# Polysketch attention into a squared-ReLU FFN: the first batch's later denominators from extra sketch columns, and its first q sketch ahead of the first FFN matmul

## The chip, the core and the metric

The kernel runs on one core of a Trainium2 chip. The metric is the device time of one execution in microseconds (us). The engines are TensorE (PE; PEld is its weight load), VectorE (DVE), ScalarE (ACT), GpSimd (POOL) and SyncE (SP, which here only issues DMAs).

## What is computed

The attention has a product feature map. Each vector x of 32 numbers is sketched by S1 and S2 into a and b of 8 numbers each, and the feature vector holds all 64 products of an entry of a with an entry of b. Its output, with the four heads side by side, is the input of a two-layer FFN with a squared ReLU.

```python
def phi(x):                                   # S1, S2: 8 x 32
    a = np.einsum('rd,bhsd->bhsr', S1, x)
    b = np.einsum('rd,bhsd->bhsr', S2, x)
    return np.einsum('bhsi,bhsj->bhsij', a, b).reshape(*x.shape[:-1], 64)
q_p, k_p = (phi(q), phi(k))                   # q, k, v: 4 batches, 4 heads, 1088 rows, 32
kv = np.einsum('bhsf,bhsd->bhfd', k_p, v)
z = np.sum(k_p, axis=2)
num = np.einsum('bhsf,bhfd->bhsd', q_p, kv)
den = np.einsum('bhsf,bhf->bhs', q_p, z)[..., None] + 1e-06
attn = num / den
x = attn.transpose(0, 2, 1, 3).reshape(4352, 128)
h = np.maximum(x @ w_in, 0.0)                 # w_in: 128 x 2048
out = h * h @ w_out                           # w_out: 2048 x 128
```

The denominator can be written in a second way: den is the sum over i of a_i(q) times (the sum over j of z_ij S2_j) applied to q. So a sketch of q with eight more columns, one for each i, gives the second factor directly.

## The kernel before

The four batches (b = 0 to 3) are pipelined: while the FFN of one batch runs, the attention of the next is made. The FFN works on chunks of columns of xT (the attention's output, 128 features by tokens). For b = 0 the chunks (list `FC`) are 256, 384 and 448 columns. Each chunk goes through 16 slices d of the hidden width: a first matmul `pg` (L615, weights `w_in`), a ReLU on ACT (L624), a square on ACT (L632) or DVE (L634), and a second matmul `po` (L653, weights `w_o`, two records each). One to four slices that fit into 512 columns are a unit. `pg` has two buffers, so the first matmuls of a unit wait for the ReLU of the unit two before.

`w_in` comes by DMA in four pieces of 512 columns, and POOL casts each piece (L689, `cast_wi`) to the type that the first matmul reads. Piece c serves the slices 4c to 4c+3: d = 0 to 3 need piece 0, d = 8 to 11 need piece 2, d = 12 to 15 need piece 3.

The attention of b = 0 has its own start, written out by hand. Its first chunk (256 tokens) is made by a short path: `kf` and `kp` (k features), `kvp` (the sums kv and z, 36 matmuls, L376), `x` (q features, L749), `bd` (kv and z as block-diagonal weights, L780), `den` and `num` (L795), then on DVE `dT` (L804), `rd`, `bc` and `xT` (L810). `a_rep` (L419) copies kv to all partitions through PE into the tile `x0`, and ACT takes it to SBUF as `kv` (L425). `keep_warm` (L696) issues matmuls whose result isn't used. The tile `x0` and the later `qc`, `kc`, `nd` and `kvp` tiles share one PSUM buffer of four banks (tag `att`, one buffer).

The rest of b = 0 is two chunks (list `AC`: (8, 12) and (20, 16), in blocks of 32 tokens; 384 and 576 tokens with padding), and b = 1 to 3 are one chunk each. For a chunk: `qT` (L289) transposes q on DVE, `qc` (L296) is the sketch on PE, six shuffles `qb` and `qa` (L506) and four products `qp` (L521) on DVE make the features, and `nd` (L538) is num on PE. The denominator is made in two ways:

- For b = 0, eight more matmuls against `z0` (L547) follow in the same PSUM tile; DVE transposes the result (`dT`, L561), adds eps (L563) and inverts it (L569). `z0` is made once by DVE (`a_rep_z`, L431) with the mask `own_c`.
- For b = 1 to 3, the sketch has eight more columns (`sw`, columns 16 to 23, made by `a_w`, L455 and L461). DVE transposes the sketch (`qt`, L469), multiplies (`pd`, L476), sums with eps (L486) and inverts (`rc`, L490). POOL then lays the result out with 16 small copies (`rd`, L497, `a_rl`).

In both cases `bc` (L575) spreads the inverse and `xT` (L584) is num times it.

Everything after the start goes through a planner (`_Order`). Each operation has an engine, a price, a key, needs, buffers and sometimes a time before which it must not start (`at`). The planner simulates the engines, takes on each free engine the ready operation with the lowest key, and emits all of it in that order. Each engine then executes its own instructions strictly in the emitted order. The operation `wi` of pieces 2 and 3 of `w_in` is one of them:

```python
for c in (2, 3):
    O.add(("wi", c), {"POOL": 0.7}, 0.5 * c, [], on(cast_wi, c), at=WI[c - 2])   # WI = (1.5, 3.0)
```

DMAs are issued by SP in program order[...].

Of the kernel before, what the change touches and what calls it, by code (L numbers as in the profile page):

```python
# [104 lines left out]
def kernel(  # L105
# [21 lines left out]
    W0, W3 = 10, 3  # L127
# [37 lines left out]
    z0 = sb("z0", 64 * H)  # L165

# [59 lines left out]
    for p in range(4):  # L226
        load_v(nc.sync, 0, p, 4, NT)
    load_wi(nc.sync, 0)
    load_wi(nc.sync, 1)
    load_q(nc.sync, 0, 256, S)  # L230
# [22 lines left out]
    own_c, own_p = sb("own_c", 32), sb("own_p", 2)  # L253
    nc.vector.memset(own_c[:], 0.0)
# [3 lines left out]
    for h in range(H):  # L258
        nc.vector.memset(own_c[32 * h : 32 * h + 32, 8 * h : 8 * h + 8], 1.0)
# [170 lines left out]
    def a_rep_z(t_, col):  # L430
        nc.vector.tensor_tensor(  # L431
            out=_ap(z0, 0, 128, 0, [[32, 4], [128, 2], [1, 32]]),
            in0=_ap(t_, 0, 128, col + 32, [[512, 4], [64, 2], [1, 32]]),
            in1=_ap(own_c, 0, 128, 0, [[0, 4], [0, 2], [1, 32]]),
            op=mult,
        )

# [10 lines left out]
    def a_qc(b, i0, nb):  # L448
        st[b, "qc", i0] = att("qc")
        sketch(st[b, "qc", i0], qT, 32 * i0, 8 * nb, sw[b % 2] if b else sf[:, 64:96])  # L450
# [14 lines left out]
    def a_qt(b, x):  # L465
        if x == 0:
            st[b, "qt"] = wpool.tile([128, 32 * NT * H], F32, tag="qt", bufs=1, name="qt")
        m = 32 * NT
        nc.vector.transpose(  # L469
            _ap(st[b, "qt"], 0, 128, 2 * m * x, [[m, 2], [1, m]]),  # L470
            banks(st[b, "qc", 0], 2 * x, 0, m),
        )

    def a_pd(b):
        qt = st[b, "qt"]
        nc.vector.tensor_tensor(  # L476
            out=_ap(pd, 0, 128, 0, [[9, 4 * NT], [1, 8]]),
            in0=_ap(qt, 0, 128, 0, [[32, 4 * NT], [1, 8]]),
            in1=_ap(qt, 0, 128, 16, [[32, 4 * NT], [1, 8]]),
            op=mult,  # L480
        )


    def a_rc(b):
        dn = wpool.tile([128, 4 * NT], F32, tag="dn", name="dn")
        nc.vector.tensor_reduce(  # L486
            out=dn[:, :], in_=_ap(pd, 0, 128, 0, [[9, 4 * NT], [1, 9]]), op=add, axis=AX
        )
        st[b, "rc"] = wpool.tile([128, 4 * NT], F32, tag="rc", bufs=1, name="rc")
        nc.vector.reciprocal(st[b, "rc"][:, :], dn[:, :])  # L490


    def a_rl(b, c):
        if c == 0:
            st[b, "rd", 0] = wpool.tile([128, 4 * NT], F32, tag="rd", name="rd")
        for h in range(H):
            nc.gpsimd.tensor_copy(  # L497
                st[b, "rd", 0][32 * h : 32 * h + 32, NT * c : NT * c + NT],
                st[b, "rc"][32 * c : 32 * c + 32, NT * h : NT * h + NT],
            )  # L500
# [26 lines left out]

    def a_nd(b, i0, nb, nd=None, col=0):
        m = 8 * nb
        nd = att("nd") if nd is None else nd  # L530
        st[b, "nd", i0] = nd, col
        kv, z = st[b, "kv"], z0
        for e in range(E):
            qp = st[b, "qp", i0, e]
            ch = [(c, h) for c in range(4) for h in range(H)]
            for c, h in ch:
                r, o = slice(32 * c, 32 * c + 32), 64 * h + 32 * e
                nc.tensor.matmul(  # L538
                    nd[32 * h : 32 * h + 32, 512 * c + col : 512 * c + col + m],
                    kv[r, o : o + 32], qp[r, m * h : m * h + m],  # L540
                    start=(e == 0), stop=(e == 1),
                )
        for o_, m0, w in dens(m) if b == 0 else ():
            for e in range(E):
                for h in range(H):
                    o = 64 * h + 32 * e
                    nc.tensor.matmul(  # L547
                        nd[32 * h : 32 * h + 32, col + o_ : col + o_ + w],
                        z[:, o : o + 32], st[b, "qp", i0, e][:, m * h + m0 : m * h + m0 + w],
                        start=(e == 0), stop=(e == 1),  # L550
                    )

    def dens(m):
        return [(m, 0, m)]

    def a_dn(b, i0, nb):
        m = 8 * nb
        (nd, col), q4 = st[b, "nd", i0], nb // 4
        dT = wpool.tile([128, 32 * NT], F32, tag="dT", bufs=1, name="dT")
        for o_, m0, w in dens(m):  # L560
            nc.vector.transpose(dT[:, m0 : m0 + w], nd[:, col + o_ : col + o_ + w])  # L561
        dn = wpool.tile([128, 4 * NT], F32, tag="dn", name="dn")
        nc.vector.tensor_scalar(  # L563
            out=_ap(dn, 0, 128, 0, [[q4, 4], [1, q4]]),
            in0=_ap(dT, 0, 128, 0, [[8, 4], [32, q4]]),
            scalar1=1e-6, scalar2=None, op0=add,
        )
        rd = st[b, "rd", i0] = wpool.tile([128, 4 * NT], F32, tag="rd", name="rd")
        nc.vector.reciprocal(rd[:, 0:nb], dn[:, 0:nb])  # L569
# [10 lines left out]
    def a_x(b, i0, nb, x, k=2):  # L580
        m = 8 * nb
        if (b, "xT") not in st:
            st[b, "xT"] = bpool.tile([128, SP], F32R, tag="xT", name="xT")
        nc.vector.tensor_tensor(  # L584
            out=_ap(st[b, "xT"], 0, 128, 32 * i0 + 2 * m * x, [[m, k], [1, m]]),
            in0=banks(st[b, "nd", i0][0], 2 * x, st[b, "nd", i0][1], m, k),
            in1=_ap(st[b, "bc", i0], 0, 128, 2 * m * x, [[m, k], [1, m]]),
            op=mult,
        )
# [137 lines left out]
    iden, irep = sb("iden", 128), sb("irep", 128)  # L727
    make_identity(nc, iden[:])
# [27 lines left out]
    a_kf(4, 3, psf, "po")  # L756
    q0(0)
# [3 lines left out]
    for t0, n in ((0, 2), (2, 2), (4, 3), (7, 2)):  # L761
        a_kp0(t0, n)
        for t in range(t0, t0 + n):
            a_kv0(t)
        if t0 == 0:
            a_kf(7, 2, psf, "po")
# [5 lines left out]
    for y in range(2):  # L772
        nc.tensor.matmul(  # L773
            den0[64 * y : 64 * y + 64, 0:256], eps[0:1, 0:64], eps[0:1, 64:320],
            start=True, stop=False,
        )

    bd = sb("bd", 256)
    for x in (1, 0):
        nc.vector.tensor_tensor(  # L780
            out=_ap(bd, 0, 128, 128 * x, [[64, 2], [32, 2], [1, 32]]),
            in0=_ap(st[0, "kvp"], 0, 128, 32 * x, [[64, 2], [0, 2], [1, 32]]),
            in1=_ap(own_p, 0, 128, 0, [[0, 2], [1, 2], [0, 32]]),
            op=mult,
        )
    st["kvt"] = wpool.tile([128, 128], F32, tag="kvt", name="kvt")
    nc.scalar.copy(st["kvt"][:, :], st[0, "kvp"][:, 0:128])
# [5 lines left out]
    for t_, x in ((den0, 1), (num0, 0)):  # L793
        for y in range(2):
# [3 lines left out]
            )  # L798
    a_rep(x0, 256)
    st["warm"] = psf.tile([128, 512], F32, tag="po", name="warm")  # L800
    keep_warm(W3)
    a_rep_kv(x0, 256)
# [10 lines left out]
    a_rep_z(x0, 256)  # L813
# [26 lines left out]
    def q_tasks(b, i0, nb, key):  # L840
# [4 lines left out]
        if True:  # L845
            for x in range(2):
# [7 lines left out]
                )  # L854
        O.add(
            ("qc", b, i0), {"PE": 0.75}, k0 - 1.0, names + [("w", b)], on(a_qc, b, i0, nb),
            rings=[("att", 1)], lag=PEL,
        )
        prev["qTuse"] = [("qc", b, i0)] if i0 + nb == 4 * NT else []
        if b:  # L860
            for x in range(2):
                O.add(
                    ("qt", b, x), {"DVE": dve(m)}, k0 - 0.3 + 0.1 * x, [], on(a_qt, b, x),
                    uses=[("qc", b, i0)], rings=[("qt", 1)] if x == 0 else [],
                )
            O.add(
                ("pd", b), {"DVE": dve(m // 2)}, k0 - 0.1, [("rc", b - 1)], on(a_pd, b),
                uses=[("qt", b, 0), ("qt", b, 1)],
            )
            O.add(  # L870
                ("rc", b), {"DVE": 0.8}, k0 - 0.1, [], on(a_rc, b), uses=[("pd", b)],
                rings=[("rc", 1)],
            )
            for c in range(4):
                O.add(
                    ("rl", b, c), {"POOL": 0.8}, k0 + 0.1 * c, [], on(a_rl, b, c),
                    uses=[("rc", b)], rings=[("rd", 2)] if c == 0 else [],
                )
# [16 lines left out]
    def nd_tasks(b, i0, nb, key):  # L895
# [3 lines left out]
            ("nd", b, i0), {"PE": 1.65 if b else 0.7 + 2.5 * max(nb, 14) / 36}, key - 3.5 - 4 * dve(m), [("kvr", b, h) for h in range(H)], on(a_nd, b, i0, nb),  # L899
            uses=qps + [("qp", b, i0, 0, 0)], rings=[("att", 1)], lag=PEL,  # L900
        )
        if b == 0:
            O.add(
                ("dn", b, i0), {"DVE": 0.72 + m / 960 / 2}, key - 3.0 - 4 * dve(m), [],
                on(a_dn, b, i0, nb), uses=[("nd", b, i0)],
            )
        for x in range(2):
            O.add(
                ("bc", b, i0, x), {"DVE": dve(m)}, key - 2.5 - 4 * dve(m) + 0.1 * x, [], on(a_bc, b, i0, nb, x),
                uses=[("dn", b, i0)] if b == 0 else [("rl", b, 2 * x), ("rl", b, 2 * x + 1)],  # L910
# [88 lines left out]
    for u in range(NU):  # L999
# [8 lines left out]
        for i in range(m):  # L1008
# [13 lines left out]
            tu[u] - 0.6, [],  # L1022
# [65 lines left out]
```

## Time and profile before

| | us |
|---|---|
| runs before: median of 4 | 189.2 (189.17 to 189.69) |
| the profiled execution | 189.12 |
| its span, first to last instruction | 187.3 |
| outside of the span | 1.8 |
| first FFN matmul (`pg`, L615) begins | 14.17 |
| first matmul of slice 12, after the first `nd` | 20.30 |
| last FFN matmuls (`pol`, L648) end in the chain | 183.35 |

The granted TensorE clock was 0.995 of full speed. Times in a timeline are from the start of the span. A line of the timeline has the start, the time, the engine, the line of the kernel, the operation, what it writes and reads, how many are merged, and in brackets the idle time of the engine before it and what ended it. A merged line covers its instructions from the first start to the last end or the sum of their times, so single instructions are shown where a duration matters.

### The profile page before, as it was taken

To read this page: it belongs to the slowest core of one execution; us is meant where nothing else is said; L and a number is where in the kernel's file an instruction comes from. 1 tells how busy PE (TensorE), PEld (TensorE's weight loads), DVE (VectorE), ACT (ScalarE), POOL (GpSimd) and SP (SyncE) were. 2 spreads that over 40 slices of the span, in tenths; PEclk is the share of its full clock that TensorE was granted. 3 is DMA by queue.
4 is the path that set the end of the run, shared out by engine and by line. 5 is a ranking of instruction groups with operands and counts; after the bars stand their busy time and mean duration, and the time that the engine had idled before them with its cause. 6 is when DMAs were issued, how large, how long until landed. Compare 5 with 4: busy or idle time off the path is not lost.

```text
span 187.3 us, 4142 instructions
## 1 busy us (share of the span) xinstructions
PE 181.9 (97%) x1586; PEld 121.9 (65%) x1587; DVE 115.3 (62%) x261; ACT 149.4 (80%) x329; POOL 28.1 (15%) x125
## 2 busy tenths in 40 slices
PE   8999999999999999999999999999999999999991
PEld 2767866666656666656577666656577656666891
DVE  4779879958992589469944589469943412222400
ACT  3418778778978989789698989789699998999960
POOL 2832000028400000085000000085000000000000
PEclk9999999999999999999999999999999999999998
DMA  5799600100039500200069200200020200020100
GB/s 178 167 334 330 161 4 2 28 3 5 0 50 267 127 7 0 44 1 2 6 138 258 37 3 0 42 4 0 5 42 0 35 0 2 8 45 0 31 11 28
DMA packets 24411, 11.27 MB, mean 60 GB/s; under 512 B 17864, under 2 KB 22728, under 8 KB 24392
## 3 DMA queue, kind: packets, MB, share of 16 engines
q1 hardware_dynamic: 23940, 10.82, 23.7%
q8 instruction: 12, 0.20, 0.4%
q10 hardware_dynamic: 452, 0.20, 0.4%
q14 instruction: 7, 0.06, 0.1%
HBM read 8.78 MB, written 2.23 MB: 59 GB/s over the span
## 4 chain that ended last, share of the span: by engine, by line
PE 94%; DMA 2%; DVE 1%; issue 0%; ACT 0%; POOL 0%; ACTq 0%; DVEq 0%
PE po L653 60%; PE pg L615 18%; PE nd L538 3%; PE kvp L394 2%; PE pol L648 2%; PE po L648 2%; PE qc L296 2%; DMA s_nat<-in_S_dram 2%; PE kvp L376 1%; PE kf L306 1%; PE kc L296 1%; PE x L749 1%; PE nd L547 1%; PE den L795 0%; PE den L773 0%
## 5 line engine op out<-in xcount | busy, mean ns | idle before, releaser
L653 PE MATMUL po<-g,w_o 128*128 128x384 f32 (+3 forms) x352 | 138.5, 478 | 0.0
L615 PE MATMUL pg<-xT,w_in 128*128 128x384 f32 (+3 forms) x192 | 110.1, 582 | 0.3 <-DVE xT L810 0.3
L624 ACT ACTIVATE gt<-pg 128x384 f32<-128x384 f32 (+4 forms) x177 | 85.2, 489 | 20.0 <-PE pg L615 16.9
L653 PEld LDWEIGHTS po<-g,w_o 128*128 128x128 f32 x352 | 62.6, 189 | 22.4 <-issue 7.3
L632 ACT ACTIVATE g<-gt 128x384 f32<-128x384 f32 (+3 forms) x138 | 71.0, 532 | 2.9
L615 PEld LDWEIGHTS pg<-xT,w_in 128*128 128x128 f32 x192 | 36.0, 190 | 24.9 <-issue 6.6
L634 DVE TENSOR_TENSOR g<-gt 128x384 f32<-128x384 f32 (+4 forms) x39 | 21.6, 556 | 39.5 <-ACT gt L624 39.4
L443 POOL COPY kv<-kvt 32x64 f32<-32x64 f32 x48 | 11.8, 246 | 90.3 <-PE po L653 63.8
L506 DVE STREAM_SHUFFLE qa<-qc 128x576 f32<-128x576 f32 (+2 forms) x20 | 11.6, 647 | 0.0
L521 DVE TENSOR_TENSOR qp<-qa,qb 128x576 f32<-128x576 f32 (+2 forms) x20 | 10.8, 598 | 0.0
L497 POOL COPY rd<-rc 32x9 f32<-32x9 f32 x48 | 8.9, 185 | 2.1
L347 DVE TENSOR_TENSOR kp<-fs 128x576 f32<-128x576 f32 x12 | 8.2, 742 | 0.0
L469 DVE STREAM_TRANSPOSE qt<-qc 128x576 f32<-128x576 f32 x6 | 4.3, 762 | 5.5 <-PE qc L296 5.5
L657 DVE STREAM_TRANSPOSE oT<-po 128x384 f32<-128x384 f32 (+3 forms) x11 | 6.2, 560 | 1.2 <-PE po L653 1.0
L538 PE MATMUL nd<-qp,kv 32*32 32x288 f32 (+2 forms) x320 | 6.8, 353 | 0.0
L338 DVE STREAM_TRANSPOSE fs<-kc 128x576 f32<-128x576 f32 x6 | 4.3, 762 | 3.9 <-PE kc L296 3.9
L538 PEld LDWEIGHTS nd<-qp,kv 32*32 32x32 f32 x320 | 3.8, 103 | 3.5 <-issue 1.7
L584 DVE TENSOR_TENSOR xT<-nd,bc 128x576 fp32r<-128x576 f32 (+2 forms) x10 | 5.6, 598 | 0.8 <-PE nd L538 0.7
L506 DVE STREAM_SHUFFLE qb<-qc 128x576 f32<-128x576 f32 (+2 forms) x10 | 6.0, 646 | 0.0
L289 DVE STREAM_TRANSPOSE qT<-qn 128x192 f32<-128x192 f32 (+3 forms) x11 | 5.8, 563 | 0.0
L696 PE MATMUL warm<-const-bfloat16-1.0 128*128 128x512 bf16 x12 | 5.0, 571 | 0.8 <-PEq L1072 0.8
L648 PE MATMUL pol<-w_o,g 128*128 128x128 f32 x32 | 5.7, 275 | 0.0
(98 smaller groups left out, 97.5 us busy)
## 6 DMA issues: line engine op xcount, KB each, us to landing
kn<-in_k_dram SPq DMA_DIRECT2D x3, 544.0 KB, 6.2
qn<-in_q_dram SPq DMA_DIRECT2D x3, 544.0 KB, 7.1
vn<-in_v_dram SPq DMA_DIRECT2D x9, 144.0 KB, 5.0
out_dram<-oT SPq DMA_DIRECT2D x24, 48.0 KB, 1.8
w_in<-in_moe_w_in_dram SPq DMA_DIRECT2D x4, 256.0 KB, 5.9
w_o<-in_moe_w_out_dram SPq DMA_DIRECT2D x4, 256.0 KB, 6.6
out_dram<-oT SPq DMA_DIRECT2D x8, 56.0 KB, 1.9
qn<-in_q_dram SPq DMA_DIRECT2D x1, 416.0 KB, 6.2
```

What stands on the lines that cost most here:

```text
L347: nc.vector.tensor_tensor(out=_ap(st[b, "kp"], 0, 128, 2 * o, [[64, NT], [8, 8], [1, 8]]), in0=_ap(fs, 0, 128, o, [[32, NT], [1, 8], [0, 8]]),
L443: nc.gpsimd.tensor_copy(_ap(st[b, "kv"], 32 * c, 32, 64 * h, [[32, E], [1, 32]]), _ap(st["kvt"], 32 * h, 32, 0, [[64, E], [1, 32]]),)
L497: nc.gpsimd.tensor_copy(st[b, "rd", 0][32 * h : 32 * h + 32, NT * c : NT * c + NT], st[b, "rc"][32 * c : 32 * c + 32, NT * h : NT * h + NT],)
L506: nc.vector.stream_shuffle(in_=banks(st[b, "qc", i0], 2 * x, 0, m), out=_ap(st[b, which, i0], 0, 128, 2 * m * x, [[m, 2], [1, m]]), mask=m ...
L521: nc.vector.tensor_tensor(out=st[b, "qp", i0, e][:, r], in0=st[b, f"qa{e}", i0][:, r], in1=st[b, "qb", i0][:, r], op=mult,)
L538: nc.tensor.matmul(nd[32 * h : 32 * h + 32, 512 * c + col : 512 * c + col + m], kv[r, o : o + 32], qp[r, m * h : m * h + m], start=(e == 0 ...
L615: nc.tensor.matmul(st["pg", u][:, n * i : n * i + n], w_in[:, 128 * (d0 + i) : 128 * (d0 + i) + 128], st[b, "xT"][:, c0 : c0 + n],)
L624: nc.scalar.activation(gt[:, 0:w], st["pg", u][:, 0:w], Relu)
L632: nc.scalar.activation(g2[:, 0:w], gt[:, 0:w], Square)
L634: nc.vector.tensor_tensor(out=g2[:, 0:w], in0=gt[:, 0:w], in1=gt[:, 0:w], op=mult)
L648: nc.tensor.matmul(po[x // 128][:, 0:128], g[:, x : x + 128], w, start=(d == 0), stop=(d == NB - 1),)
L653: nc.tensor.matmul(po[0][:, 0:n], w, g, start=(d == 0), stop=(d == NB - 1))
```

## The change

1. **Denominators of the two later chunks of b = 0.** The eight matmuls against `z0`, `z0` itself, the mask `own_c`, and the DVE steps `dT`, add and reciprocal go. Instead the chunks take the way of the other batches: `qc` reads `sw[0]` with eight more columns, then `qt`, `pd`, `rc` on DVE and 16 copies `rl` on POOL for each of the two chunks.
2. **How the extra columns of b = 0 are made.** DVE transposes S2 into `s2f`, `zm` is z with a mask `own_f`, four small matmuls of `s2f` and `zm` go into columns 384 to 391 of `x0`, and ACT copies them to `sw[0]`.
3. **The first q sketch.** `qT` and `qc` of the chunk (8, 12) are issued in the hand-written start: `qT` on DVE before `bd`, `qc` on PE between two `keep_warm` matmuls, ahead of the first `pg`. Three `keep_warm` matmuls become two.
4. **Order of the start.** `kf` of the k tiles 7 and 8 goes ahead of the q features on PE; `kvt` is copied by DVE instead of ACT; `num` goes behind `a_rep`; POOL makes the identity earlier. The second q load is cut in two, and its first part (256 to 640, 192 KB) goes ahead of the first two `w_in` pieces on SP.
5. **Keys.** The squares of the first two units get a much earlier key.

The planner makes a new order from this. On POOL it puts the 16 copies of the chunk (8, 12) ahead of the cast of piece 3 of `w_in`; the cast of piece 2 stays ahead of them:

```
w_in<-w_in 128x512 x3
rd<-rc 32x3 x16
w_in<-w_in 128x512
rd<-rc 32x4 x16
```

On DVE the chunk (8, 12) reads: `xT`, `qt` x2, `pd`, squares 128x256 x2, sum, reciprocal, `qb` x2, `qa` x4, `qp` x4, `bc`, a square 128x512, `bc`, `qT` x2, `xT` x2. On PE, the first `nd` stands behind the same FFN matmuls as before (12 `pg`, 5 `po`), and the second `nd` and what follows it for b = 1 one slice later.

```diff
+    load_q(nc.sync, 0, 256, 640)
     load_wi(nc.sync, 0)
     load_wi(nc.sync, 1)
-    load_q(nc.sync, 0, 256, S)
+    load_q(nc.sync, 0, 640, S)
...
-    own_c, own_p = sb("own_c", 32), sb("own_p", 2)
+    own_p = sb("own_p", 2)
...
+    iden, irep = sb("iden", 128), sb("irep", 128)
+    make_identity(nc, iden[:])
+    own_f, s2f, zm = sb("own_f", 16), sb("s2f", 32), sb("zm", 32)
+    nc.vector.tensor_reduce(
+        out=own_f[:, :], in_=_ap(iden, 0, 128, 0, [[8, 16], [1, 8]]), op=add, axis=AX
+    )
...
-        sketch(st[b, "qc", i0], qT, 32 * i0, 8 * nb, sw[b % 2] if b else sf[:, 64:96])
+        sketch(st[b, "qc", i0], qT, 32 * i0, 8 * nb, sw[b % 2])
...
-    def a_rl(b, c):
+    def a_rl(b, i0, nb, c):
+        n = nb // 4
         if c == 0:
-            st[b, "rd", 0] = wpool.tile([128, 4 * NT], F32, tag="rd", name="rd")
+            st[b, "rd", i0] = wpool.tile([128, 4 * NT], F32, tag="rd", name="rd")
         for h in range(H):
             nc.gpsimd.tensor_copy(
-                st[b, "rd", 0][32 * h : 32 * h + 32, NT * c : NT * c + NT],
-                st[b, "rc"][32 * c : 32 * c + 32, NT * h : NT * h + NT],
+                st[b, "rd", i0][32 * h : 32 * h + 32, n * c : n * c + n],
+                st["rc"][32 * c : 32 * c + 32, n * h : n * h + n],
             )
...
-        for o_, m0, w in dens(m) if b == 0 else ():
-            for e in range(E):
-                for h in range(H):
-                    o = 64 * h + 32 * e
-                    nc.tensor.matmul(
-                        nd[32 * h : 32 * h + 32, col + o_ : col + o_ + w],
-                        z[:, o : o + 32], st[b, "qp", i0, e][:, m * h + m0 : m * h + m0 + w],
-                        start=(e == 0), stop=(e == 1),
-                    )
...
     a_kf(4, 3, psf, "po")
+    a_kf(7, 2, psf, "pg")
     q0(0)
     q0(1)
...
-        if t0 == 0:
-            a_kf(7, 2, psf, "po")
+
+    nc.vector.transpose(s2f[:, :], _ap(sf, 0, 128, 72, [[0, 4], [1, 8]]))
...
+    for i0 in (8, 14):
+        a_qT(0, i0, 6)
...
+    a_bd(1)
     st["kvt"] = wpool.tile([128, 128], F32, tag="kvt", name="kvt")
-    nc.scalar.copy(st["kvt"][:, :], st[0, "kvp"][:, 0:128])
+    nc.vector.tensor_copy(st["kvt"][:, :], st[0, "kvp"][:, 0:128])
+    nc.vector.tensor_tensor(
+        out=_ap(zm, 0, 128, 0, [[16, 2], [8, 2], [1, 8]]),
+        in0=_ap(st[0, "kvp"], 0, 128, 32, [[64, 2], [0, 2], [1, 8]]),
+        in1=_ap(own_f, 0, 128, 0, [[0, 2], [8, 2], [1, 8]]),
+        op=mult,
+    )
+    a_bd(0)
...
+    nd0(den0, 1)
+    for h in range(H):
+        nc.tensor.matmul(
+            x0[32 * h : 32 * h + 32, 384:392], s2f[:, :], zm[:, 8 * h : 8 * h + 8],
+            skip_group_check=True,
+        )
     a_rep(x0, 256)
+    nc.scalar.copy(sw[0][:, 16:24], x0[:, 384:392])
+    a_rep_kv(x0, 256)
+    nd0(num0, 0)
     st["warm"] = psf.tile([128, 512], F32, tag="po", name="warm")
     keep_warm(W3)
-    a_rep_kv(x0, 256)
+    a_qc(0, *AC[0][1])
+    keep_warm(W4)
...
-    a_rep_z(x0, 256)
...
-        if b:
-            for x in range(2):
+        for x in range(2):
...
-                    ("rl", b, c), {"POOL": 0.8}, k0 + 0.1 * c, [], on(a_rl, b, c),
-                    uses=[("rc", b)], rings=[("rd", 2)] if c == 0 else [],
+                ("rl", b, i0, c), {"POOL": 0.8}, k0 + 0.1 * c, [], on(a_rl, b, i0, nb, c),
+                uses=[("rc", b, i0)], rings=[("rd", 2)] if c == 0 else [],
...
-            tu[u] - 0.6, [],
+            tu[u] - (0.6 if u > 1 else 40.0), [],
```

## The prediction

> **What bounds the kernel now.** First the page's busy times and its chain.
>
> ```profile
> PE 181.9 (97%) x1586; PEld 121.9 (65%) x1587; DVE 115.3 (62%) x261; ACT 149.4 (80%) x329; POOL 28.1 (15%) x125
> PE 94%; DMA 2%; DVE 1%; issue 0%; ACT 0%; POOL 0%; ACTq 0%; DVEq 0%
> ```
>
> From the first FFN matmul to the end, PE issues almost without a hole, so the end follows from when PE begins, what it must issue, and where it has to wait. Next, the timeline of the start and of the two `nd` blocks.
>
> ```profile
> 9.27 1.85 PE L376 MATMUL kvp<-vn,kp 128*64 128x64 f32 x56
> 11.17 0.49 DVE L780 TENSOR_TENSOR bd<-kvp,own_p 128x128 f32<-128x128 f32 x2 [0.26 <-PE kvp L376]
> 12.33 0.45 DVE L804 STREAM_TRANSPOSE dT<-den 128x256 f32<-128x256 f32 x1 [0.67 <-PE den L795]
> 13.29 0.37 ACT L425 COPY kv<-x 128x256 f32<-128x256 f32 x1 [1.28 <-PE x L419]
> 14.17 0.71 PE L615 MATMUL pg<-xT,w_in 128*128 128x256 f32 x4 [0.26 <-DVE xT L810]
> ...
> 18.94 0.96 PE L538 MATMUL nd<-qp,kv 32*32 32x96 f32 x64
> 19.83 0.54 PE L547 MATMUL nd<-qp,z 128*32 128x96 f32 x16
> 20.30 0.39 PE L615 MATMUL pg<-xT,w_in 128*128 128x256 f32 x1
> ...
> 33.50 1.07 PE L538 MATMUL nd<-qp,kv 32*32 32x128 f32 x64
> 34.50 0.65 PE L547 MATMUL nd<-qp,z 128*32 128x128 f32 x16
> 35.07 0.44 PE L615 MATMUL pg<-xT,w_in 128*128 128x384 f32 x1
> ```
>
> The reader sees a chain `kvp`, `bd`, `den`, `dT`, `xT`, `pg`, 3.00 us from `bd` (11.17) to the first `pg` (14.17), and that the matmuls against `z` hold PE from 19.83 to 20.30 and from 34.50 to 35.07. The `pg` at 20.30 is slice 12, the first that reads piece 3 of `w_in`. Last, how POOL and DVE disturb each other.
>
> ```profile
> 14.77 0.61 POOL L689 CAST w_in<-w_in 128x512 fp32r<-128x512 f32 x1 [2.49 <-DMA w_in<-in_moe_w_in_dram]
> 14.98 0.68 DVE L634 TENSOR_TENSOR g<-gt 128x256 f32<-128x256 f32 x1
> ...
> 45.66 3.59 POOL L497 COPY rd<-rc 32x9 f32<-32x9 f32 x16
> ...
> 82.53 0.46 DVE L476 TENSOR_TENSOR pd<-qt 128x288 f32<-128x288 f32 x1
> 82.53 0.55 POOL L443 COPY kv<-kvt 32x64 f32<-32x64 f32 x1
> ```
>
> The square of 256 columns met the cast and ended 0.28 after it (15.38 to 15.66); the next one took 0.41. The POOL copy met `pd` and took 0.55, where 40 of its kind take about 0.23. The 16 copies took 3.59 beside shuffles alone.
>
> [...]
>
> **The change part by part.** Sums are made against the profiled execution (189.12 us, span 187.3), 0.08 below the median of 189.2.
>
> *Start, up to `bd`.* Four `kf` records move ahead of the q features: 0.112 each (14 in 1.6) is 0.45, so these begin at 7.45 and not 7.00, and `kvp` 1.07 later, at 8.52. Its 72 records at 0.0297 (56 from 9.27 to 10.90) issue the last at 10.63, 0.27 earlier than 10.90. `bd` could begin at 10.90. DVE must be done with `kp`, `s2f`, `qp` and two `qT` by then: `kp` by 9.05, `qp` after ACT's `qb` (which ends at 9.22) by 9.9, `qT` 0.6. This holds if the q slice lands by 10.25. It is issued at 6.15, where the first `w_in` piece is issued now; that lands 4.85 later with 256 KB. [...] I take no loss; at worst it lands at 10.8 and costs 0.5. The pieces of `w_in` come about 0.6 later (casts at 11.65 and 12.25 in place of 11.04 and 11.67), still ahead of the first `pg`. The earlier identity on POOL, `own_f` and fewer memsets lie in idle time before the k load lands (DVE idle to 3.54).
>
> *From `bd` to the first `pg`.* DVE's chain would still give 3.00: the `kvt` copy, `zm` and the second `bd` are done 0.85 after the first `bd`, and `dT` waits for `den` to 1.16. But PE now has a longer queue before `pg`. `den` runs from 0.46 to 0.94 after `bd` (as now), the four small matmuls to 1.25 (no row; 0.1 to 0.5, I take 0.2[...]), `a_rep` to 1.68 (0.43), then `num` and one `warm`. `qc` needs the PSUM buffer of `x0`, so it waits for ACT: the new copy of 8 columns (0.2) and `kv` (0.37), from 1.88 to 2.4. `qc` takes 0.56 (14.81 to 15.37) from 2.55, the last `warm` 0.21: `pg` at about 3.35. With `bd` at 10.90 this is 14.25, **+0.08**. Bounds: 3.0 (hidden) to 3.6.
>
> *`qc` out of the FFN.* It frees 0.56 of PE behind slice 3. This buys nothing: the fifth unit's `pg` (17.00) waits for ACT's third-unit ReLU, and ACT runs without a gap from 14.56 to 18.9. The first `nd` is reached 4.6 to 4.7 us after the first `pg`, now 4.77.
>
> *DVE to `nd`.* `z` (0.33 of pitch) and `qT` (0.63) go out from between `xT` and the squares; `qt` (0.63), `pd`[...], the sum (0.27 from 0.49 less 216 elements) and the reciprocal (0.23, as L569) come in: +0.4. `nd` may start some 0.1 us later than now; its second half waits for the last product, 5.1 us after `pg`.
>
> *POOL, the dear part.* The cast of piece 3 (0.61, now 16.14 to 16.75) stands behind the 16 copies, and the copies behind `rc`. From the first `pg`: `qt` to 0.65; `pd` meets the cast of piece 2 (still 14.77 to 15.38) and ends at 1.4; squares to 1.95, sum and reciprocal to 2.35. Copies from 2.4 at 0.224 (3.59/16; three elements instead of nine save next to nothing, as 64 elements take 0.27). Seven are done when the products `qp`, which have two SBUF inputs, begin at 3.95. If copies and products take turns, four more are done by 5.15. Then `bc`, and a square of 512 (two inputs[...]) beside the rest: the last copy ends at 6.7, the cast at 7.3, slice 12 starts at 7.4. Now it is 6.13 (20.30 less 14.17). PE alone, with 0.47 of matmuls against `z` gone, would be there at 5.7. So PE waits some 1.7, and the first block's saving turns into **+1.2**. [...] if the products and the square shut POOL out altogether 8.5 (+2.4).
>
> *Second block.* The matmuls against `z` go: 35.07 less 34.50, **-0.57**. DVE gets `qt`, `pd`, sum and reciprocal (1.5) for `dT`, add, reciprocal (0.73). This is hidden: `xT` of this chunk is due six slices of 0.82 later, `bc` no longer waits for `nd`, and DVE is ahead because the first chunk's `xT` comes about a microsecond sooner. The 16 copies have 4.9 us until `nd`. If that cover went, it would cost at most the added 0.8. For b = 1, `nd` stands four slices of 0.95 ahead of its first use in place of five, for 1.53 of `nd` and 1.42 of `xT`: no loss.
>
> Sum: 0.08 + 1.2 - 0.57 = +0.7; 189.82 for the execution, **189.9** on the median.
>
> **Rivals.**
> - *Shut out* (0.20): products and square run back to back and POOL gets nothing between them. For it: `pd` held a copy to its very end. Against it: one instruction isn't a row of them. 0.08 + 2.4 - 0.57 = +1.9: 191.1.
> - [...] (0.22): `pd` misses the cast, and copies slip in between. 0.08 + 0.2 - 0.57 = -0.3: 188.9; half of this reads as no change.
> - *PE sets the pace* (0.13), the faster side: slice 12 starts when `nd` ends, since the copies start over a microsecond before my date or cost 0.1 in place of 0.224. The point from which it decides: the cast over by 5.6 us after the first `pg`. Then both blocks count, 0.47 and 0.57: -1.0, 188.2. Against it: 16 copies at 0.224 and the cast are 4.2, and `rc` is not ready before 1.9.
> - *Late q slice* (0.05): `qT` holds `bd`, +0.4 on top of the forecast: 190.3. For it: slow DMA from 7.5 to 10.
>
> **How the numbers follow.** The forecast has 0.40 and its own range 189.6 to 190.6. A comparison of this kernel can tell about 0.2% (0.38 us). Faster by more: the third rival and half of the second less a bit, 0.21. Within: the rest of the second and the forecast's edge, 0.19. Slower: 0.60. The range from 188.6 to 191.2 leaves out most of the third rival and the far end of the first.
>
> **What would show it.** Right: POOL's casts as three, then 16 small copies, then one at about 21 us; PE idle before slice 12, released by POOL; the first `pg` near 14.25; no L547; 0.57 less around the second `nd`. Wrong: slice 12 straight behind `nd`, a first `pg` off by over 0.3, or a new wait behind the second `nd`.

## The result, and the profile after

The changed kernel takes 189.78 us (median of 44 runs, 189.15 to 193.1) against 189.19 for the kernel before. The ratio of the mean times is 1.0047, 95% interval 1.0034 to 1.006: slower by half a per cent, which is 0.89 us. The profiled execution of after took 189.33, 0.21 more than that of before.

That median hides the shape. 23 runs lie between 189.15 and 189.79 (median 189.42) with a mean granted TensorE clock of 0.997 to 1.000, the upper-clock group; 18 lie between 190.75 and 191.6 (median 190.97) with a clock of 0.989 to 0.991, the lower-clock group; nothing lies between. Executions more than 1.5% above the fastest of their kernel, here three near 193 at a full clock and five of the 62 of the kernel before (193.2 to 195.5), are left out of the ratios here and below. The median of 189.78 is the mean of the two longest runs of the upper-clock group; had two of its runs fallen into the other group, it would be near 190.8. The kernel before has no group 1.5 us above its usual one. So two questions stand: what the schedule cost (0.2 us in the profiled execution), and what costs another 1.55 us in two runs of five.

The profiled execution of after belongs to the upper-clock group. Its busy times, its chain, and its costliest first-matmul group:

```profile
PE 180.0 (96%) x1561; PEld 120.8 (64%) x1562; DVE 116.9 (62%) x264; ACT 148.8 (79%) x328; POOL 36.3 (19%) x157
PE 91%; POOL 2%; DVE 2%; DMA 2%; issue 1%; ACT 0%; ACTq 0%; DVEq 0%; POOLq 0%
L581 PE MATMUL pg<-xT,w_in 128*128 128x384 f32 (+3 forms) x192 | 110.6, 584 | 2.0 <-POOL w_in L655 1.5
```

The same group of first matmuls before:

```profile
L615 PE MATMUL pg<-xT,w_in 128*128 128x384 f32 (+3 forms) x192 | 110.1, 582 | 0.3 <-DVE xT L810 0.3
```

PE shows 25 records fewer, and is no longer 94% but 91% of the chain; POOL, which was not in it, has entered, and the first matmuls now show 2.0 us of idle time (before: 0.3), 1.5 of them released by POOL's cast of `w_in`. The timeline of after shows where (one row is a start, a duration, the engine and the operation):

```profile
10.92 0.29 DVE L748 TENSOR_TENSOR bd<-kvp,own_p 128x128 f32<-128x128 f32 x1 [0.39 <-PE kvp L379]
13.92 0.79 PE L581 MATMUL pg<-xT,w_in 128*128 128x256 f32 x4
...
14.79 0.26 DVE L470 TENSOR_TENSOR pd<-qt 128x96 f32<-128x96 f32 x1
15.93 0.23 DVE L484 RECIPROCAL rc<-dn 128x12 f32<-128x12 f32 x1
16.23 4.26 POOL L492 COPY rd<-rc 32x3 f32<-32x3 f32 x16 [1.36 <-DVE rc L484]
20.55 0.61 POOL L655 CAST w_in<-w_in 128x512 fp32r<-128x512 f32 x1
...
18.78 0.96 PE L531 MATMUL nd<-qp,kv 32*32 32x96 f32 x64
21.21 0.38 PE L581 MATMUL pg<-xT,w_in 128*128 128x256 f32 x1 [1.47 <-POOL w_in L655]
...
35.40 1.07 PE L531 MATMUL nd<-qp,kv 32*32 32x128 f32 x64
36.40 0.91 PE L619 MATMUL po<-g,w_o 128*128 128x384 f32 x2
```

The first `pg` starts at 13.92 instead of 14.17. The first `nd` group is over in under a microsecond, with no matmuls against `z` behind it, but the cast of piece 3, whose rows were issued at 9.19 and landed 6.9 later (16.1), waits until 20.55 for the 16 copies that stand ahead of it on POOL, and slice 12 (21.21) for the cast: 20.30 before, so the kernel is now 0.91 late. At the second `nd` the FFN goes on 1.00 after its start (35.40 to 36.40), where it took 1.57 (33.50 to 35.07). The last matmuls of the chain end at 183.66 instead of 183.35.

### The profile page after: what moved, and what is told of

It is laid out like the page before. It is cut to its first block, busy times and chain, and to the rows that moved or that the text cites. A ratio compares the mean times of both kernels' runs of the same rounds, so it can differ in the third digit from the quotient of the medians.

```text
span 187.5 us, 4132 instructions
## 1 busy us (share of the span) xinstructions
PE 180.0 (96%) x1561; PEld 120.8 (64%) x1562; DVE 116.9 (62%) x264; ACT 148.8 (79%) x328; POOL 36.3 (19%) x157
## 4 chain that ended last, share of the span: by engine, by line
PE 91%; POOL 2%; DVE 2%; DMA 2%; issue 1%; ACT 0%; ACTq 0%; DVEq 0%; POOLq 0%
PE po L619 59%; PE pg L581 17%; PE nd L531 3%; PE kvp L397 2%; POOL rd L492 2%; PE pol L614 2%; PE po L614 2%; PE qc L299 2%; DMA s_nat<-in_S_dram 2%; PE kvp L379 1%; PE kf L309 1%; PE kc L299 1%; PE x L713 1%; DVE qt L464 0%; POOL w_in L655 0%
## 5 line engine op out<-in xcount | busy, mean ns | idle before, releaser
L600 DVE TENSOR_TENSOR g<-gt 128x384 f32<-128x384 f32 (+4 forms) x40 | 22.1, 553 | 39.9 <-ACT gt L590 39.9
L492 POOL COPY rd<-rc 32x9 f32<-32x9 f32 (+2 forms) x80 | 17.1, 213 | 13.9 <-DVE rc L484 10.5
L464 DVE STREAM_TRANSPOSE qt<-qc 128x576 f32<-128x576 f32 (+2 forms) x10 | 5.8, 615 | 6.2 <-PE qc L299 6.1
L541 DVE STREAM_TRANSPOSE bc<-rd 128x576 f32<-128x576 f32 (+2 forms) x10 | 5.7, 604 | 0.8 <-POOL rd L492 0.8
```

The lines of the kernel that those rows point to most:

```text
L492: nc.gpsimd.tensor_copy(st[b, "rd", i0][32 * h : 32 * h + 32, n * c : n * c + n], st["rc"][32 * c : 32 * c + 32, n * h : n * h + n],)
L600: nc.vector.tensor_tensor(out=g2[:, 0:w], in0=gt[:, 0:w], in1=gt[:, 0:w], op=mult)
```

## The experiments

Each kernel below is compared with runs of the kernel before that were made beside it (medians 189.22 to 189.26). Three explanations were under test. *Cast theory*: the cast behind the copies costs the first block what the second saves. *Port theory* (a name only, no run here shows a port): the copies are long because VectorE's two-input instructions run beside them. *Gap theory* for the lower group: TensorE's empty 1.5 us before slice 12 sets off a stretch at a lower clock in part of the executions; its rival, *head theory*, is that the thinner filler in the head (two filler matmuls where there were three) does it.

### The cast ahead of the copies

```diff
+seq.remove(wi); seq.insert(seq.index(by_name["rl", 0, 8, 0]), wi)   # emitted order only; wi = ("wi", 3)
```

> The fourth cast of w_in stands ahead of the sixteen copies of the first batch's second chunk on GpSimd instead of behind them; nothing else moves. Cast theory (the copies hold the cast, the cast holds slice 12, and that costs the first block what the second one saves): TensorE no longer waits 1.5 us for GpSimd, slice 12 follows the nd group at about 19.6 instead of 21.2; the copies end 0.6 later (about 21.1), which the second xT can take since its chunk is due later; 187.9 to 188.5 us in the usual executions. Rival, ScalarE paces this stretch: the wait moves to a relu or a square and at most 0.3 us is won, 189.0 or more. On the second group of times that the changed kernel shows (about 191, clock .99), gap theory (TensorE's empty 1.5 us sets off a stretch at a lower clock in part of the executions): that group is gone. Head theory (the thinner filler before the first FFN matmul does it): the group stays, about 1.6 us above the usual times, in some two of five executions.

Measured: 188.13 us (188.01 to 188.25 in eight of ten runs), ratio 0.9948 (0.9933 to 0.9962): better than both kernels. Slice 12 follows `nd` at once, and no run has a clock below 0.996: with the wait the lower-clock group is gone too. The profiled execution was slower than the others (189.47), and its timeline says why:

```profile
17.33 0.62 POOL L655 CAST w_in<-w_in 128x512 fp32r<-128x512 f32 x1 [2.59 <-DMA w_in<-in_moe_w_in_dram]
17.89 4.06 POOL L492 COPY rd<-rc 32x3 f32<-32x3 f32 x16
...
19.82 0.38 PE L581 MATMUL pg<-xT,w_in 128*128 128x256 f32 x1
23.60 0.41 PE L581 MATMUL pg<-xT,w_in 128*128 128x384 f32 x1 [1.31 <-DVE xT L550]
```

Here the cast could not begin before 17.33, when piece 3 had landed (16.14 in the profile of before); all copies stood behind it, and the second chunk's `xT` came 1.31 late. That the eight faster runs had an earlier landing is inferred from their times. One queue with two customers: in the changed kernel the copies hold the cast until 20.55, here the cast holds the copies until 17.89.

### The empty stretch filled, whole and by half

```diff
+if u == 7: keep_warm(10, 384, nd[:, 1664:2048])   # bf16 filler into unused columns, ahead of slice 12
```

> The changed kernel with ten filler matmuls (bf16, 384 columns, into unused columns of the nd tile) behind the nd group, so that TensorE is busy while it waits for the fourth cast; the wait itself stays. Gap theory: the usual times stay at 189.2 to 189.8 (slice 12 still at about 21.2) and the group at about 191 is gone. Head theory: both groups stay with the shares they had. If the filler outlasts the cast, up to 0.2 us more.

Measured: 189.32, ratio 1.0005 (0.9997 to 1.0013). Twelve of 13 runs lie between 189.17 and 189.74, one at 193.12; none near 191. The filler runs from 19.64 until slice 12 starts at 21.17 (21.21 without it). The wait for the cast is unchanged; only the group at 191 has gone.

```diff
-keep_warm(10, 384, nd[:, 1664:2048])
+keep_warm(5, 384, nd[:, 1664:2048])
```

> The changed kernel with five filler matmuls behind the nd group instead of ten, so that TensorE's empty stretch before slice 12 is about 0.75 us instead of 1.6. Gap theory, with the share growing with the gap: the group at 191 in one or two of ten executions or none; a fixed share, whatever the length: two of five. Head theory: two of five.

Five fillers in place of ten leave 0.54 of wait. Measured: 189.28, ratio 1.0001 (0.9993 to 1.0009); all 13 runs between 189.04 and 189.69. Of the 25 runs with filler in the usual range none is in the lower-clock group, of 41 without 18 are. The fillers leave the wait for the cast as it was, and both kernels are even with the kernel before within their intervals, whose upper ends are 0.17 and 0.25 us: **the change's own schedule costs a quarter of a microsecond at most; most of the half per cent is the clock.**

### A third filler in the head

```diff
-W0, W3, W4 = 10, 1, 1
+W0, W3, W4 = 10, 2, 1
```

> The changed kernel with a third filler matmul in the head again (two before the q sketch instead of one), so that the head has as many as the kernel before; the 1.5 us wait for the fourth cast stays. Head theory: the group at about 191 is gone, all usual times at 189.2 to 189.8. Gap theory: the group stays, some two of five executions near 191.

Measured: of 19 runs five lie from 189.46 to 189.96 and eight from 190.97 to 191.23 at a clock of 0.990 or 0.991, ratio 1.0063 (1.0045 to 1.0082); the other six lie near 193 at a full clock, and why they are so many here stays open. The group stays, so the head theory falls. The profiled execution (191.23, clock 0.990) is one of that group. Its view by stretch of time (busy time and, in brackets, instructions of each engine, then the granted clock, the DMA share and GB/s):

```profile
18.00:20.00 2.00, 1.94 (x70) 1.28 (x68) 1.97 (x7) 1.97 (x4) 1.78 (x6) 1.00 1.10 210
20.00:21.00 1.00, 0.00 (x0) 0.00 (x0) 0.28 (x1) 0.06 (x1) 0.81 (x5) 1.00 1.13 233
21.00:22.00 1.00, 0.59 (x2) 0.52 (x3) 1.00 (x5) 0.00 (x0) 0.35 (x1) 0.83 0.83 279
22.00:25.00 3.00, 3.00 (x10) 2.53 (x9) 1.46 (x3) 1.23 (x2) 0.00 (x0) 0.50 0.08 21
25.00:26.00 1.00, 1.00 (x7) 0.89 (x6) 0.33 (x1) 0.85 (x2) 0.00 (x0) 0.97 0.00 0
```

PE does nothing from 20 to 21 (its wait here is 1.47 us, as in the changed kernel), and a quarter of a microsecond after slice 12 starts (21.41) its clock is halved: 0.34 us of the third row (0.17 lost at half speed), 3.0, and 0.06 of the fifth, 3.40 in all. Half of that, 1.70, is lost, and the two groups of the changed kernel lie 1.55 apart. This is the only trace of a lower-clock run; that the others had the same stretch is inferred from their clocks, since 1.70 lost of 189.4 makes a mean of 0.991. Two matmuls show it one by one, the same `po` pair at full clock and in the stretch:

```profile
18.46 0.59 PE L619 MATMUL po<-g,w_o 128*128 128x256 f32 x2
22.67 1.05 PE L619 MATMUL po<-g,w_o 128*128 128x256 f32 x2
```

### The kernel before with such a gap

```diff
+seq.remove(wi); seq.insert(seq.index(by_name["nd", 0, 8]) + 1, wi)   # emitted order; wi = ("wi", 3)
...
+if c == 3:                                   # before its cast of piece 3
+    nc.gpsimd.tensor_copy(own_p[:, 0:1], qp[:, 288:289])
+    for _ in range(4): cast_wi(4)            # the same piece again
```

> The kernel before, with its fourth cast of w_in held back: a GpSimd copy that needs the last qp product and four further casts of the same piece stand ahead of slice 12, so that TensorE is empty for some 1.7 us between the nd group and slice 12 (slice 12 at about 22.0 instead of 20.3). Head and filler are those of the kernel before. Gap theory: usual times at about 190.8 (189.2 + 1.7) and a second group about 1.6 us above them, near 192.4, at a clock of about .99. Head theory: one group only, at about 190.8.

Measured: 191.22, 191.24, 191.25, 191.35, 192.49 and 193.19, ratio 1.0133 (1.0103 to 1.0164); in the profiled execution (191.35) the wait was 2.00, and the usual time is 189.26 + 2.0 as it should be. The two longest have a clock of 0.987 and 0.988, the other four of 0.996 to 0.998; of the 75 runs of the kernel before beside these experiments none is below 0.994. So a gap put into the kernel before, with its own head, brings runs at a lower clock as well, as the gap theory has it and the head theory does not. Six runs are too few to give a share, and the two times (1.2 and 1.9 above the rest) make no sharp second group.

### The new start alone

```diff
+a_rep_z(x0, 256)
...
+for o_, m0, w in dens(m) if b == 0 else ():     # the z matmuls behind nd, and a_dn, as before
...
-for x in range(2):
-    O.add(("qt", b, i0, x), ...)
+if b:                                           # qt, pd, rc, rl for b = 1 to 3 alone
+    for x in range(2):
+        O.add(("qt", b, i0, x), ...)
```

> The new start alone: first q sketch ahead of the first FFN matmul, new head, but the denominators of both later chunks of the first batch by the z matmuls as in the kernel before; no copies stand in the cast's way. Cast theory: the first pg at about 13.9 to 14.2 and no wait for a cast at slice 12; second nd again with its z matmuls; 188.7 to 189.1 us. Gap theory: one group of times only, since TensorE has no empty 1.5 us. Head theory: a second group about 1.6 us above the first in some two of five executions, since the thinner filler is in this kernel too.

Measured: 189.86, ratio 1.0033 (1.0021 to 1.0045); all six runs from 189.7 to 189.93. A miss: 188.7 to 189.1 had been expected. There is no wait at slice 12, but the early sketch waits 0.71 for VectorE's `z`, because `qc` needs the PSUM buffer of `x0`, which `z` reads:

```profile
14.01 0.46 PE L303 MATMUL qc<-qT,sw 32*32 32x96 f32 x32 [0.71 <-DVE z L439]
14.44 0.83 PE L621 MATMUL pg<-xT,w_in 128*128 128x256 f32 x4
```

The first `pg` comes 0.27 later than in the kernel before (14.17). Of the 0.6 us by which this kernel is slower that is less than half; the rest was not located. As placed here, then, a sketch ahead of the first FFN matmul costs time where `z` is kept; whether it gains any where `z` is gone was not run by itself. The six runs in one group, with the thin head, are one more mark against the head theory.

### The cast between the copies

```diff
-seq.insert(seq.index(by_name["rl", 0, 8, 0]), wi)   # ahead of the first copy
+seq.insert(seq.index(by_name["rl", 0, 8, 2]), wi)   # ahead of the ninth
```

> The fourth cast stands between the eighth and the ninth copy. Cast theory: it runs at about 18.2 to 18.9, before slice 12 needs it (19.6), whether its rows landed at 16 or at 17.3; the copies end 0.6 later than in the changed kernel, about 21.1; xT of the second chunk is ready near 22.4, TensorE wants it near 22.2. About 188.1 us, as with the cast ahead of all copies, and without the 1.3 us stall that the profiled execution of that kernel showed (its rows landed late and held all sixteen copies, 189.47). Rival, the copies' end is what counts and the chunk stalls for xT by some 0.5: 188.5.

Measured: 188.57 (188.45 to 188.7), ratio 0.9961 (0.9949 to 0.9973), near the rival. Its timeline has the cast beside the four products:

```profile
17.79 1.57 DVE L516 TENSOR_TENSOR qp<-qa,qb 128x192 f32<-128x192 f32 x4
18.24 0.63 POOL L655 CAST w_in<-w_in 128x512 fp32r<-128x512 f32 x1
21.19 0.38 DVE L541 STREAM_TRANSPOSE bc<-rd 128x192 f32<-128x192 f32 x1 [0.97 <-POOL rd L492]
22.80 0.41 PE L581 MATMUL pg<-xT,w_in 128*128 128x384 f32 x1 [0.56 <-DVE xT L550]
```

The four products in the changed kernel, with copies but no cast beside them:

```profile
17.74 1.16 DVE L516 TENSOR_TENSOR qp<-qa,qb 128x192 f32<-128x192 f32 x4
```

Slice 12 is free (19.79). The cast met the four products, which took 1.57 instead of 1.16. That is not what made `xT` late, though: VectorE then stood idle for 0.97 us until the copies were done, at 21.16 instead of 20.49, so the second `bc` began at 21.19 instead of 20.52 and `xT` was 0.56 late. The end of the copies is what counts, as the rival had it.

```diff
+for x in (0, 1): move("x", 0, 8, x) ahead of ("qT", 0, 20)   # with the cast between the copies
```

> As the cast between the copies, and both xT products of the second chunk stand ahead of the two q transposes of the third on VectorE (0.66 us). Cast theory: xT ready near 21.8, before TensorE wants it; 187.8 us if the chunk still waited in the kernel without this, 188.1 if it did not. Rival: the q sketch of the third chunk comes late by 0.6 and TensorE or VectorE waits there, 188.3 or more.

Measured: 188.85 (188.45 to 188.94 in four runs), ratio 0.9967 (0.9954 to 0.998). The wait for `xT` is gone, but PE now reaches the k sketch `kc` before VectorE has finished the k transposes `kT` (at 24.25), and waits there instead:

```profile
23.74 1.33 PE L301 MATMUL kc<-kT,sf 32*32 32x288 f32 x32
```

It takes 1.33 in place of 0.77, and the first matmul behind it starts 4.90 after slice 12, against 4.92 without the move. The rival's number held, though the k sketch, not the q sketch, paid.

### The square on ScalarE

```diff
-square(u, eng)
+square(u, "ACT" if u == 5 else eng)
```

> The changed kernel with one square of 512 columns (slices 8 and 9, VectorE at 19.11) given to ScalarE, nothing else. Port theory (a copy of GpSimd's took 0.60 us beside that square instead of 0.18 to 0.23[...]): the copies end 0.4 earlier (near 20.1), the cast too, slice 12 at about 20.8 instead of 21.2, TensorE's empty stretch 1.2 us; 188.9 us in the upper-clock executions. Rival, [...] copies end at 20.5 as before, no gain; ScalarE's extra 0.6 may cost 0.2. Gap theory: with 1.2 us empty instead of 1.6 the share of executions near 191 falls below the two of five.

Measured: 188.85, ratio 0.9983 (0.9974 to 0.9992). The view of the copies, first a copy beside the square in the changed kernel, and that square:

```profile
19.21 0.60 POOL L492 COPY rd<-rc 32x3 f32<-32x3 f32 x1
19.11 0.66 DVE L600 TENSOR_TENSOR g<-gt 128x512 f32<-128x512 f32 x1
```

and without the square:

```profile
19.25 0.18 POOL L492 COPY rd<-rc 32x3 f32<-32x3 f32 x1
16.48 3.84 POOL L492 COPY rd<-rc 32x3 f32<-32x3 f32 x16 [1.28 <-DVE rc L484]
21.05 0.38 PE L581 MATMUL pg<-xT,w_in 128*128 128x256 f32 x1 [1.31 <-POOL w_in L655]
```

The 16 copies take 3.84 instead of 4.26: one copy was held 0.42 by the square. The wait shrank less, from 1.47 to 1.31, since this execution began its copies 0.25 later. Eleven runs are in one group, 188.69 to 189.36, and two near 192.5 at a full clock; the lower-clock group was not met. The 1.31 is the wait of one execution (189.15), among the longest of the eleven, so the others may have waited less.

### The versions that beat both

```diff
+move("wi", 3) ahead of ("rl", 0, 8, 0)
+for i in (20, 28): move("qT", 0, i) ahead of ("bc", 0, 8, 1)
```

> The fourth cast ahead of all sixteen copies, and the two q transposes of the third chunk (0.66 us of VectorE) ahead of the second bc of the second chunk, where VectorE stood idle for GpSimd's copies (0.75 us in the changed kernel, 0.97 with the cast between the copies). Cast theory: no wait at slice 12, and xT of the second chunk comes right after bc, 0.6 earlier than with the cast ahead alone; 187.6 to 188.1 us, below the 188.13 of that kernel if its usual executions still waited for xT. Rival, that wait was not on the path there: 188.1 again. If the fourth piece lands late (17.3 instead of 16), some 0.7 of stall remains.

Measured: 188.12 (187.69 to 189.32, six runs), ratio 0.9939 (0.9924 to 0.9955); in the profiled execution (189.32) piece 3 landed late again, its cast at 17.66, and `xT` was 1.18 late. So the piece's load was moved too:

```diff
 load_wi(nc.sync, 2)
-load_wo(nc.sync, 1)
 load_wi(nc.sync, 3)
+load_wo(nc.sync, 1)
```

> As the cast ahead and the q transposes first, and the load of the fourth piece of w_in stands one place further ahead on SyncE's queue, before the second piece of w_out. Cast theory with the landing as its limit: the cast runs at about 15.0 to 15.6, always before the copies may start (16.2), so the copies never wait for it; 187.5 to 187.9 us with a narrower spread. Rival: the second piece of w_out lands 0.8 us later and holds the po matmuls of slices 4 to 7 (wanted from about 17): no gain, 188.0 or more.

Measured: 187.77 (187.67 to 188.04), ratio 0.9929 (0.9917 to 0.9942), the best that was found, though the interval overlaps that of the version without the earlier load. The timeline: two casts done by 15.4, copies not held by them, no wait at slice 12 or at the second chunk.

```profile
14.17 1.26 POOL L657 CAST w_in<-w_in 128x512 fp32r<-128x512 f32 x2 [1.60 <-DMA w_in<-in_moe_w_in_dram]
16.71 4.25 POOL L494 COPY rd<-rc 32x3 f32<-32x3 f32 x16 [1.28 <-DVE rc L486]
19.91 0.38 PE L583 MATMUL pg<-xT,w_in 128*128 128x256 f32 x1
22.03 0.51 PE L583 MATMUL pg<-xT,w_in 128*128 128x384 f32 x1
```

With the square on ScalarE (the edit shown above) on top:

> Cast ahead, q transposes first, the fourth piece loaded earlier, and the square of 512 columns on ScalarE. If the copies' end is still what the second xT waits for: 0.4 earlier, 187.3 to 187.7 us. If ScalarE, which has the squares before it, is what the po matmuls of slices 8 to 11 then wait for: 0.3 to 0.6 worse than the same kernel with the square on VectorE.

Measured: 187.85 (187.65 to 187.87 in four runs), ratio 0.9926 (0.9913 to 0.994): the same as without the square on ScalarE. With no cast behind the copies, their earlier end (19.89 instead of 20.96 in the profiled executions) bought nothing.

## Why the prediction was right, and where it was not

The number, 189.9 against 189.78, is better than the reasons behind it, and that is luck: the schedule by itself gave 189.42, below the range of 189.6 to 190.6, and a loss of clock that was not forecast moved the median to the upper edge of the upper-clock group.

- *Start.* `bd` at 10.92, predicted 10.90: the count of the `kf` and `kvp` records held. `bd` to `pg` was 3.00, predicted 3.35: the mis-sized terms are `qc` and the last `warm`. `qc` began 2.56 after `bd` (13.48; predicted 2.55), but the next start came 0.38 later instead of 0.56, and the `pg` 0.06 after the last `warm` instead of 0.21. That is level with DVE's chain (`xT` ends 0.15 before the first `pg` in both kernels), the lower bound given. First `pg`: -0.25, not +0.08.
- *DVE.* `rc` was done 2.24 after the first `pg`, predicted 2.35. `pd` took 0.26 for its 96 products (0.46 for 288 in the kernel before); it hardly met the cast of piece 2, which had come earlier (14.25 instead of 14.77).
- *POOL.* The last copy ended 6.57 after the first `pg` (20.49), predicted 6.7; slice 12 began after 7.29, predicted 7.4; PE's wait was "some 1.7" and is 1.47. This was the heart of the forecast, and it held: four copies began while the four products ran, which took 1.16 beside them and 1.15 in the kernel before with none. Where a GpSimd instruction and a two-input VectorE instruction met, either of the two took longer: with the cast between the copies the products took 1.57 beside the cast for 1.16, and in the changed kernel a copy took 0.60 beside the square for 0.18 without it. First block, 7.29 less 6.13: +1.16, predicted +1.2 (7.4 less 6.13 is nearer 1.3). The cause, the cast behind the copies, is shown by the kernel with the cast ahead.
- *Second block.* -0.57, to the hundredth, and the added DVE work was hidden.
- *Sum.* -0.25 + 1.16 - 0.57 = +0.34; measured at the end of the chain +0.31, in time +0.21. Predicted +0.7. As a schedule the change gains nothing and costs little, by the filled kernels too (1.0001 and 1.0005).
- *The step that failed* is the clock, for which the sum has no term. With the wait that the forecast itself had (some 1.7, measured 1.47) the clock is lower, 0.989 to 0.991, in two runs of five. 18 of 41 times 1.55 is 0.68 in the mean, which together with +0.21 is the 0.89 us of the measured 0.47%. The prediction had 0.33 too much at the start and left this out; the two errors met.

Of the rivals, *PE sets the pace* named the right condition (the cast over before `nd` ends): once an experiment met it, 188.13 came out where 188.2 had been worked out. *Shut out* did not occur, and the second rival neither: the 16 copies took 4.26, where 16 beside shuffles alone took 3.59 in the kernel before. *Late q slice* did not occur: the q transposes ran at 9.90, without a wait.

## What to carry to other kernels

When work is moved onto a slack engine, look at what is queued behind it there, and put the instruction that the critical engine waits for first, with its load early enough that it doesn't hold the rest. Count a new hole on TensorE not only by its length: in this kernel one of 1.47 us also came with a lower clock in 18 of 41 runs, and in none of 25 with five or ten filler matmuls in it, which cost nothing that shows (1.0001 and 1.0005 of the kernel before). Look at all the times, not at a median: two groups 1.5 us apart were the best clue here.

## What the runs showed of the hardware

- A hole in TensorE's work between a group of small matmuls and full ones, 1.47 us in the profiles, came with a lower mean clock (0.989 to 0.991) in 26 of 54 runs of two kernels (18 of 41 and 8 of 13); one of 2.00, put into the kernel before, did in two of six. The one trace of such a run has 3.40 us at half clock, beginning a quarter of a microsecond after the hole (slice 12 starts at 21.41). Why only part of the executions are hit was not shown. In the kernels whose profiles show 0.54 of wait (13 runs) and 1.31 (11 runs) the group was absent. Whether it is the idle time alone, or also the light `nd` matmuls before it, was not tried.
- The landing of a piece of `w_in` behind the same queue wandered by more than a microsecond: the cast that it releases began at 16.32 (the new start alone), 17.33 (the cast ahead) and 17.66 (with the q transposes first) in three kernels with the same loads. The profiled executions of the last two, where the cast stood ahead of all copies, took 189.47 and 189.32, over a microsecond more than the medians of their kernels.
